# More tiles for rounded weight pieces, a product queue one shorter, and another order of first sums in an attention, expert and gated kernel

## The chip, the cores and the metric

The kernel runs on one core of one Trainium2 chip. The metric is the device time of one execution in microseconds (us); lower is better. Shown times are medians of several runs, and one further execution was recorded by the hardware profiler. Engines are written as the profile writes them: PE (TensorE matmuls), PEld (its weight loads), DVE (VectorE), ACT (ScalarE), POOL (GpSimd), SP (the queue that issues most DMAs).

## The reference

Three layers follow one another; float32 in and out (the weights come as float64, their bits are taken apart on the chip).

```python
# 1. attention with sigmoid weights: 4 batches, 12 heads, 448 tokens, 64 per head
scores = scale * np.matmul(q, k.transpose(0, 1, 3, 2)) - np.log(S)
x = np.matmul(1 / (1 + np.exp(-scores)), v)      # -> 1792 tokens x 768
# 2. top-1 mixture of 8 experts, 768 -> 1024 -> 768, routed by cosine similarity
out[mask] = gate_w[mask, None] * (np.maximum(x[mask] @ w1[e], 0) @ w2[e])
# 3. gated layer, 768 -> 1536 -> 768: the last part of the kernel
a = x @ w_a
b = x @ w_b
return (a * b @ w_out).astype(np.float32)
```

## The kernel before

The change lies in the last part, the function `glu`. The 1792 rows of x go through it in two groups of 896 rows (`G` = 2). For each group, first the two products x @ w_a and x @ w_b are made and multiplied for 12 slices of 128 hidden columns (`ab`, one call for each slice, `f`), and the result is sent to DRAM (`m_d`). Then `out_part` multiplies it with `w_out` in two passes of 12 steps each (`k` from 0 to 23): four blocks of 128 rows in the first pass, three in the second.

**Splitting.** A float32 product is made of three matmuls of rounded pieces. `split` does it: ACT casts the source to the high piece (L718), DVE subtracts it from the source to get the low piece (L719).

**Seven products.** The two products of one slice are done by a scheme with seven block products instead of eight (`NPROD` = 7). `combo(n)` prepares the weight operand of product n: for product 1 two sums in a row, for products 3 and 6 one sum each (`sum_`, L1020, on DVE), for products 0, 2, 4 and 5 none, and then a split. Product 6's combo also starts the load of a later weight slice (`w_load`, L1009, on SP). The operands lie in a pool of 10 `w` tiles; `ab` prepares each operand `AHEAD` = 8 products before it is used, at the head of the product's turn in the loop. Since the scheme has seven products, in product j of `ab` the combo of number (j + 1) mod 7 stands. After each product DVE takes sums out of PSUM: `u2` after product 1 (L1061), `u3` after product 3 (L1066, L1067), `c21` and half of `m` after product 5 (L1072, L1073), the rest after product 6 (L1079, L1080). Three PSUM banks serve seven products (`BANK`), so product 3 may begin only when `u2` has been read, and product 5 when `u3` has.

**The right-hand operand.** `y_combo(g, c)` makes one column block (of seven) of x's group g: six transposes on PE, one copy `k1` on ACT (L981), two casts on ACT (L987, L988), four first sums on DVE into `ts` (L989 to L992), a cast of these on ACT (L993), and three subtractions on DVE (L995 to L997). The seven columns of group 0 are made one after the other ahead of the first `ab`, a combo behind each. Those of group 1 are made inside `out_part(0)` at the steps k in `rows_at`, a row load (`y_next`) some steps ahead of each.

**Rounded pieces of w_out.** While `ab` runs for group 0, `prep_more` is called in product 2 and in product 5 of each slice. A call stores what an earlier call finished (`prep_store`, L218, on SP), finishes the unit of an earlier call on DVE (`prep_finish`, L211), starts a load, and begins a new unit (`prep_unit`): two steps on DVE (L195, L197), two on ACT (L199, and L201, an absolute value written into a tile `ab`), one addition on POOL (L202). A unit is finished two calls after it was begun and stored three calls after. There are three `ab` tiles, so the unit begun in that third later call writes the tile which the store issued in that same call is reading.

Each engine takes its instructions in the order in which the program issues them (a schedule by hand), and waits on semaphores.

Of the kernel before, what the change touches and what calls it, by code (L numbers as in the profile page):

```python
# [9 lines left out]
F32 = mybir.dt.float32  # L10
F32R = mybir.dt.float32r
# [13 lines left out]
def build(ctx: ExitStack, tc: tile.TileContext, q, k, v, emb, tau, w1, w2, wa, wb, wo, out, dbg=None, stop=None):  # L25
# [6 lines left out]
    nc = tc.nc  # L32
# [4 lines left out]
    P = 128  # L37
# [6 lines left out]
    HD = DM // 2  # L44
# [19 lines left out]
    prep_p = prep_s.enter_context(tc.tile_pool(name="prep", bufs=1))  # L64
# [8 lines left out]
    G = len(PHASES)  # L73
# [91 lines left out]
    HU = DM // 2  # L165
    units = [(f, part, hf) for parts in ((0, 1), (2,)) for f in range(NF) for part in parts for hf in range(2)]
    next_unit, unit_end = [0], [4 * NF]
    prep_raw = {}
    prep_sum, prep_out = [], []

    def prep_load(u, dma=nc.sync):
        if u >= unit_end[0]:
# [12 lines left out]
    def prep_unit():  # L185

        u = next_unit[0]
        if u not in prep_raw:
            return
        next_unit[0] += 1  # L190
        t = prep_raw.pop(u)
        top, low = t[:, :, 1], t[:, :, 0]
        t16 = t.rearrange("p n t -> p (n t)").bitcast(BF16).rearrange("p (n t) -> p n t", t=4)[:, :, 3]
        m = prep_p.tile([P, HU], I32, tag="m", name="m", bufs=2)
        nc.vector.tensor_scalar(out=m, in0=top, scalar1=3, scalar2=0x3FFFFFFF,  # L195
                                op0=ALU.logical_shift_left, op1=ALU.bitwise_and)
        nc.vector.scalar_tensor_tensor(out=m, in0=top, scalar=-0x40000000, in1=m,  # L197
                                       op0=ALU.bitwise_and, op1=ALU.bitwise_or)
        nc.scalar.activation(out=low, in_=low.bitcast(U32), func=AF.Copy, scale=2.0 ** -29)  # L199
        ab = prep_p.tile([P, HU], F32, tag="ab", name="ab", bufs=3)  # L200
        nc.scalar.activation(out=ab, in_=t16, func=AF.Abs)  # L201
        nc.gpsimd.tensor_tensor(out=m, in0=m, in1=low, op=ALU.add)  # L202
        prep_sum.append((u, m, ab))
# [479 lines left out]
    HP = P // 2  # L683
    yg = {}

    def y_load(g, c, tiles):

        w = DM // len(tiles)
        for h in range(2):
            r0 = Y0 * (1 - g) + (h * NC + c) * HP  # L690
            for hf, t in enumerate(tiles):
                nc.sync.dma_start(out=t[h * HP:(h + 1) * HP, :], in_=ys_d[r0:r0 + HP, hf * w:(hf + 1) * w])
        yg[g, c] = tiles if len(tiles) == 2 else [tiles[0][:, :HD], tiles[0][:, HD:]]
# [15 lines left out]
    def transpose_raw(px, t, k0, n):  # L709

        px = px.bitcast(F32R)
        t = t.bitcast(F32R)
        for kk in range(n):
            nc.tensor.transpose(out=px[:, kk * P:(kk + 1) * P], in_=t[:, (k0 + kk) * P:(k0 + kk + 1) * P],
                                identity=ident_r)
# [228 lines left out]
    def glu():  # L944
# [4 lines left out]
        def pool(name, bufs, **kw):  # L949
            return gs.enter_context(tc.tile_pool(name=name, bufs=bufs, reuse_waits="tile", **kw))  # L950

        g_p = pool("g", 1)
        ps_o = pool("ps_o", 1, space=PSUM)
        ps_y = pool("ps_y", 2, space=PSUM)
        KH = KD // 2
        HN = NC * HP
        B11, B21, B22, T1, T2, T3, T4 = range(7)
# [1 line left out]
        RHS = [B11, T2, T1, T3, B21, T4, B22]  # L959
        BANK = [0, 1, 2, 1, 0, 1, 2]  # L960
        NPROD = 7
        AHEAD = 8
        NS = G * NF
        bt = [g_p.tile([P, 7, KH, HN], F32R, name=f"bt{h}") for h in "hl"]

        def tmp(tag, n, bufs, nm, dt=F32):
            return g_p.tile([P, 512], F32, tag=tag, name=nm, bufs=bufs)[:, :n]

        def acc_ps(k):
            return [ps_o.tile([P, 512], F32, tag=f"o{3 * k + j}", name=f"o{3 * k + j}") for j in range(3)]  # L970


        def y_combo(g, c, px=None):

            px = [ps_y.tile([P, 512], F32, tag="py", name="py") for _ in range(2)] if px is None else px
            hv = yg.pop((g, c))
            k = [t[:, :HD] for t in px]
            for hf in range(2):
                transpose_raw(k[hf], hv[hf], 0, KH)
            k1 = tmp("c21", HD, 1, "k1")  # L980
            nc.scalar.copy(out=k1, in_=k[0])  # L981
            v = [a.rearrange("p (k h q) -> p h k q", k=KH, h=2) for a in (k1, k[1])]
            t = g_p.tile([P, 4, KH, HP], F32, tag="ts", name="ts", bufs=1)
            cs = slice(c * HP, (c + 1) * HP)
            sub = ALU.subtract
            bh, bl = (b[:, :, :, cs] for b in bt)
            nc.scalar.copy(out=bh[:, B11], in_=v[0][:, 0])  # L987
            nc.scalar.copy(out=bh[:, B21:B22 + 1], in_=v[1])  # L988
            nc.vector.tensor_tensor(out=t[:, 0], in0=v[0][:, 1], in1=v[0][:, 0], op=sub)  # L989
            nc.vector.tensor_tensor(out=t[:, 1], in0=v[1][:, 1], in1=t[:, 0], op=sub)  # L990
            nc.vector.tensor_tensor(out=t[:, 2], in0=v[1][:, 1], in1=v[0][:, 1], op=sub)
            nc.vector.tensor_tensor(out=t[:, 3], in0=v[1][:, 0], in1=t[:, 1], op=sub)  # L992
            nc.scalar.copy(out=bh[:, T1:], in_=t)  # L993
            bf = bh.bitcast(F32)
            nc.vector.tensor_tensor(out=bl[:, B11], in0=v[0][:, 0], in1=bf[:, B11], op=sub)  # L995
            nc.vector.tensor_tensor(out=bl[:, B21:B22 + 1], in0=v[1], in1=bf[:, B21:B22 + 1], op=sub)
            nc.vector.tensor_tensor(out=bl[:, T1:], in0=t, in1=bf[:, T1:], op=sub)  # L997

        def y_next(g, c):
            t = g_p.tile([P, DM], F32, tag="yr", name="yr", bufs=2)  # L1000
            y_load(g, c, [t])


        def w_raw(i):
            return r2[0][:, 2 * (i % 4):2 * (i % 4) + 2, :]
# [7 lines left out]
        def combo(n):  # L1013
            i, j = divmod(n, NPROD)
            r = w_raw(i)
            a1, a2, b1, b2 = (r[:, s, hf * HD:(hf + 1) * HD] for s in range(2) for hf in range(2))

            def sum_(k, x, y, op):
                t = g_p.tile([P, HD], F32, tag=f"s{min(k, 3)}", name=f"s{k}", bufs=1)
                nc.vector.tensor_tensor(out=t, in0=x, in1=y, op=op)  # L1020
                sums[k] = t

            if j == 1:
                sum_(1, b1, b2, ALU.add)
                sum_(2, sums[1], a1, ALU.subtract)
            elif j == 3:
                sum_(3, a1, b1, ALU.subtract)
            elif j == 6:
                sum_(4, a2, sums[2], ALU.subtract)
            src = sums[S_OF[j]] if S_OF[j] else {0: a1, 4: a2, 5: b2}[j]  # L1030
            w = g_p.tile([P, 2, HD], F32R, tag="w", name="w", bufs=10)
            split(w[:, 0], w[:, 1], src, w[:, 0].bitcast(F32))
            wq[n] = w
            if j == NPROD - 1:
                w_load(i + 4)


        def ab(i):
# [6 lines left out]
            for j in range(NPROD):  # L1045
                n = i * NPROD + j
                if n + AHEAD < (g + 1) * NF * NPROD:
                    combo(n + AHEAD)
                w = wq.pop(n)
# [42 lines left out]
        op, accs = {}, []  # L1092
# [11 lines left out]
        def out_split(g, k):  # L1104
            if k < 2 * NF:
                mr, wr = op[g, k]
                n = mr.shape[-1]
                gh, gl = (tmp(tg, n, 2, nm).bitcast(F32R) for tg, nm in (("p1", "gh"), ("u2", "gl")))
                wh, wl = (g_p.tile([P, 2, HD], F32R, tag="w", name="w", bufs=10).rearrange("p a b -> p (a b)")
                          for _ in range(2))  # L1110
                split(gh, gl, mr, gh.bitcast(F32))
                split(wh, wl, wr, wh.bitcast(F32))
                op[g, k] = (gh, gl, wh, wl)
# [38 lines left out]

        def out_part(g):

            rows_at = {3: 0, 5: 1, 7: 2, 9: 3, 12: 4, 15: 5, 18: 6} if g + 1 < G else {}
            for k in range(2 * NF):
                out_load(g, k + 2) if k + 2 < 2 * NF else None
                out_split(g, k + 1)
                if rows_at and k < 2 * NF:
                    c = next((c for kk, c in rows_at.items() if kk == k + 3), None)  # L1160
                    if c is not None:
                        y_next(g + 1, c)
                out_mm(g, k)
                store(g)
                if k in rows_at:
                    y_combo(g + 1, rows_at[k])
                elif k < 3:
                    prep_more(g)
                if g + 1 < G and 14 <= k < 14 + AHEAD:
                    combo((g + 1) * NF * NPROD + k - 14)  # L1170

        for i in range(4):
            w_load(i)
        y_next(0, NC - 1)
        for c in range(NC):
            y_combo(0, c, acc_ps(c % 3)[:2] if c % 3 < 2 else None)
            combo(c)
        unit_end[0] = len(units)
        for u in range(next_unit[0], next_unit[0] + 3):
            prep_load(u)  # L1180
        for n in range(NC, AHEAD):
            combo(n)
# [50 lines left out]
```

## Time and profile before

| | us |
|---|---|
| median of 3 runs | 1155.24 (1155.08 to 1155.33) |
| the profiled execution's own time | 1152.64 |
| its span in the profile | 1150.9 |
| PE busy | 1059.7 (92%) |
| DVE busy | 734.3 (64%) |
| ACT busy | 504.4 (44%) |
| mean granted TensorE clock | 0.962 of full speed |

Busy time of an engine is the share of the span in which it executes; instructions that only wait or issue a DMA are not counted. A row of a timeline gives start, duration, engine, line and operands, and in square brackets how long the engine sat idle just before and what released it. The granted clock is 1.00 at 2.4 GHz and 0.50 at 1.2 GHz. The part `glu` runs from about 553 us to the end.

### The profile page before, as it was taken

The page shows a single profiled execution, that of the slowest core. Times are in us where ns is not written, and L with a number is a line of the kernel's source. Part 1 is how long each engine was busy: PE and PEld are TensorE (multiplying, and loading weights), DVE is VectorE, ACT ScalarE, POOL GpSimd, SP SyncE. Part 2 cuts the span into 40 slices and gives each one's busy share as a digit, 9 for nine tenths or more (in the row PEclk, how much of TensorE's full clock was granted, in tenths as well). Part 3 has the DMA queues.
Part 4 walks back from the last instruction along what each step waited for, and adds up shares of the span by engine and source line. Part 5 has one row for each costly group of instructions (what it writes and reads, how often), then busy time and mean ns, then how long its engine had stood idle before and what let it go on. Part 6 is the DMA issues. An engine that isn't in the chain of part 4 may idle for free.

```text
span 1150.9 us, 17128 instructions
## 1 busy us (share of the span) xinstructions
PE 1059.7 (92%) x5780; PEld 876.2 (76%) x5780; DVE 734.3 (64%) x1399; ACT 504.4 (44%) x841; POOL 150.9 (13%) x218
## 2 busy tenths in 40 slices
PE   7999999999999999999468798889998999999998
PEld 4555555699888888898357687787886899998887
DVE  2465788756956695631586777775666677775444
ACT  5776677424845483512343323332544222232343
POOL 2121213132222222211001111110000000000000
PEclk9999999999999999999678988989998999999999
DMA  8577687546877687151433434436574222203564
GB/s 194 147 187 201 179 230 221 197 158 252 304 267 253 256 309 277 67 140 42 154 124 125 159 134 125 165 119 213 160 238 139 101 88 107 78 37 127 166 208 150
DMA packets 129468, 195.58 MB, mean 170 GB/s; under 512 B 52040, under 2 KB 92616, under 8 KB 129360
## 3 DMA queue, kind: packets, MB, share of 16 engines
q1 hardware_dynamic: 125392, 179.14, 48.8%
q0 software_dynamic: 3040, 14.94, 3.4%
q8 instruction: 47, 0.77, 0.3%
q14 instruction: 61, 0.50, 0.1%
q10 hardware_dynamic: 928, 0.23, 0.1%
HBM read 151.02 MB, written 43.25 MB: 169 GB/s over the span
## 4 chain that ended last, share of the span: by engine, by line
PE 33%; DVE 8%; ACT 4%; DMA 3%; issue 3%; SPq 0%; DVEq 0%; ACTq 0%
PE o L1053 22%; PE o L1134 11%; DVE w L719 2%; DMA wo<-ab 2%; ACT w L718 2%; DVE s L1020 1%; ACT bth L993 1%; DVE btl L997 1%; DMA wr<-wo 1%; DVE u L1061 1%; DVE ts L990 0%; ACT k L981 0%; ACT p L1058 0%; DMA raw<-in_moe_w_out_dram 0%; DVE gl L719 0%
## 5 line engine op out<-in xcount | busy, mean ns | idle before, releaser
L1053 PE MATMUL o<-bth,w 128*128 128x448 f32 x1008 | 302.6, 380 | 36.8 <-DVE u L1061 27.5
L1053 PEld LDWEIGHTS o<-bth,w 128*128 128x128 f32 x1008 | 198.5, 197 | 58.7 <-issue 30.7
L1053 PE MATMUL o<-btl,w 128*128 128x448 f32 x504 | 191.0, 379 | 1.1 <-DVE btl L995 1.1
L1134 PE MATMUL o<-w,gh 128*128 128x512 f32 (+1 forms) x672 | 174.8, 349 | 11.5 <-ACT w L718 6.5
L1134 PEld LDWEIGHTS o<-w,gh 128*128 128x128 f32 x672 | 118.2, 194 | 32.8 <-DVE w L719 10.5
L202 POOL TENSOR_TENSOR m<-m,raw 128x384 int32<-128x384 int32 x72 | 74.8, 1039 | 496.8 <-DVE m L197 233.7
L718 ACT CAST w<-s 128x384 fp32r<-128x384 f32 x96 | 49.2, 513 | 196.4 <-DVE s L1020 176.1
L1134 PE MATMUL o<-w,gl 128*128 128x512 f32 x336 | 116.9, 348 | 1.4 <-DVE gl L719 1.4
L1053 PEld LDWEIGHTS o<-btl,w 128*128 128x128 f32 x504 | 99.4, 197 | 9.9 <-DVE btl L995 1.5
L530 ACT ACTIVATE a<-ps,bias_s 112x896 f32<-112x896 f32 x96 | 91.6, 1005 | 30.8 <-PE ps L529 30.4
L719 DVE TENSOR_TENSOR w<-s,w 128x384 fp32r<-128x384 f32 x96 | 53.6, 558 | 54.4 <-ACT w L718 54.4
L780 PE MATMUL p<-w1h,xl 128*128 128x512 f32 x216 | 85.3, 395 | 2.6 <-DVE xl L719 2.6
L778 PE MATMUL p<-w1h,xh 128*128 128x512 f32 x216 | 86.6, 401 | 0.1
L779 PE MATMUL p<-w1l,xh 128*128 128x512 f32 x216 | 84.6, 392 | 0.0
L541 PE MATMUL av<-a,v 112*64 112x448 f32 x384 | 82.5, 552 | 0.0
L864 PE MATMUL p<-w2h,hTl 128*128 128x384 f32 x288 | 74.1, 338 | 8.3 <-DVE hTl L719 8.3
L201 ACT ACTIVATE ab<-raw 128x384 f32<-128x384 bf16 x72 | 39.8, 553 | 90.3 <-DMA wo<-ab 46.4
L864 PE MATMUL p<-w2h,hTh 128*128 128x384 f32 x288 | 76.2, 345 | 0.0
L719 DVE TENSOR_TENSOR hTl<-px,hTh 128x512 fp32r<-128x512 f32 x35 | 24.1, 688 | 81.4 <-ACTq L845 68.1
L864 PE MATMUL p<-w2l,hTh 128*128 128x384 f32 x288 | 73.6, 336 | 0.0
L1134 PEld LDWEIGHTS o<-w,gl 128*128 128x128 f32 x336 | 65.3, 194 | 10.3 <-DVE gl L719 2.6
L719 DVE TENSOR_TENSOR gl<-mr,gh 128x512 fp32r<-128x512 f32 (+1 forms) x48 | 29.9, 623 | 50.1 <-ACT gh L718 49.8
(246 smaller groups left out, 1771.9 us busy)
## 6 DMA issues: line engine op xcount, KB each, us to landing
r<-in_moe_w_dram SPq DMA_DIRECT2D x28, 768.0 KB, 7.8
r<-in_moe_w_dram SPq DMA_DIRECT2D x18, 1024.0 KB, 6.2
r<-wab SPq DMA_DIRECT2D x24, 768.0 KB, 4.4
wr<-wo SPq DMA_DIRECT2D x48, 384.0 KB, 3.6
m<-mm SPq DMA_DIRECT2D x24, 448.0 KB, 2.5
raw<-in_moe_w_a_dram SPq DMA_DIRECT2D x24, 384.0 KB, 3.5
raw<-in_moe_w_b_dram SPq DMA_DIRECT2D x24, 384.0 KB, 5.0
wab<-ab SPq DMA_DIRECT2D x48, 192.0 KB, 3.7
```

The lines of the kernel that those rows point to most:

```text
L201: nc.scalar.activation(out=ab, in_=t16, func=AF.Abs)
L202: nc.gpsimd.tensor_tensor(out=m, in0=m, in1=low, op=ALU.add)
L530: nc.scalar.activation(out=a[:, c2], in_=ps[:, :, :S], func=AF.Sigmoid, bias=bias_s[:CP], scale=qscale)
L541: nc.tensor.matmul(t[j * D:(j + 1) * D, :S], lhsT=raw[i, "v"][:, j, c, :], rhs=a[:, c2, j, :], start=c == 0, stop=c == NCH - 1)
L718: nc.scalar.copy(out=hi, in_=src)
L719: eng.tensor_tensor(out=lo, in0=src, in1=f32_hi, op=ALU.subtract)
L778: nc.tensor.matmul(ps, lhsT=xh[:, kk, :], rhs=w1h[kk][:, cs], start=kk == 0, stop=False)
L779: nc.tensor.matmul(ps, lhsT=xh[:, kk, :], rhs=w1l[kk][:, cs], start=False, stop=False)
L780: nc.tensor.matmul(ps, lhsT=xl[:, kk, :], rhs=w1h[kk][:, cs], start=False, stop=kk == KD - 1)
L864: nc.tensor.matmul(yp[hf][:, :HD], lhsT=l[:, kk, :], rhs=wv[kk][:, hf * HD:(hf + 1) * HD], start=kk == 0 and wv is w2h and l is hTh, stop= ...
L1053: nc.tensor.matmul(bank[BANK[j]], lhsT=w[:, l, ks], rhs=bt[r][:, RHS[j], kk, :], start=j < 3 and kk + l + r == 0, stop=kk == KH - 1 and l ...
L1134: nc.tensor.matmul(t[:, z0:z0 + d1 - d0], lhsT=l[:, cs], rhs=r[:, d0:d1], start=first and z == 0, stop=last and z == 2)
```

## The change

Five things are done together.

- Two more tiles for the absolute values (`ab2`, in another pool), used by two units of every five in the last part, so that a tile is used again after five units and not three.
- `AHEAD` is 7 and not 8, and there are 9 `w` tiles and not 10. In product j of `ab` now the combo of number j stands.
- `y_combo` is divided into `y_sums` (transposes, copy, casts, first sums) and a rest (cast of the sums, three subtractions). Ahead of group 0's products the rest of a column is issued behind the first sums of the next one; `k1` and the sums alternate between two tiles for that.
- Group 1's columns are made at steps 1, 3, 5, 7, 9 of the first pass and 12, 16 of the second, instead of 3, 5, 7, 9 and 12, 15, 18. The first row load is issued at the head of `out_part`.
- At step 1 a column stands where `prep_more` stood.

```diff
@@ prep_unit
-        ab = prep_p.tile([P, HU], F32, tag="ab", name="ab", bufs=3)
+        ab = (prep_p.tile([P, HU], F32, tag="ab", name="ab", bufs=3) if not more_ab or u % 5 < 3 else
+              more_ab[0].tile([P, HU], F32, tag="ab2", name="ab2", bufs=2))
@@ glu
-        AHEAD = 8
+        AHEAD = 7
@@ y_combo, now y_sums, which returns rest
-            k1 = tmp("c21", HD, 1, "k1")
+            k1 = tmp(*(("c21", HD, 1, "k1") if c % 2 else ("p1", HD, 2, "k1")))
-            t = g_p.tile([P, 4, KH, HP], F32, tag="ts", name="ts", bufs=1)
+            t = g_p.tile([P, 4 * KH * HP if ts == "ts" else 2 * HN], F32, tag=ts, name=ts, bufs=1)
+            t = t[:, :4 * KH * HP].rearrange("p (s k q) -> p s k q", s=4, k=KH)
-            nc.scalar.copy(out=bh[:, T1:], in_=t)
...
+            def rest():
+                nc.scalar.copy(out=bh[:, T1:], in_=t)
+                nc.vector.tensor_tensor(out=bl[:, B11], in0=v[0][:, 0], in1=bf[:, B11], op=sub)
+                nc.vector.tensor_tensor(out=bl[:, B21:B22 + 1], in0=v[1], in1=bf[:, B21:B22 + 1], op=sub)
+                nc.vector.tensor_tensor(out=bl[:, T1:], in0=t, in1=bf[:, T1:], op=sub)
@@ combo, and the same in out_split
-            w = g_p.tile([P, 2, HD], F32R, tag="w", name="w", bufs=10)
+            w = g_p.tile([P, 2, HD], F32R, tag="w", name="w", bufs=9)
@@ out_part
-            rows_at = {3: 0, 5: 1, 7: 2, 9: 3, 12: 4, 15: 5, 18: 6} if g + 1 < G else {}
+            rows_at = {1: 0, 3: 1, 5: 2, 7: 3, 9: 4, 12: 5, 16: 6} if g + 1 < G else {}
+            if rows_at:
+                y_next(g + 1, 0)
@@ ahead of group 0's products
+        rest = None
         for c in range(NC):
-            y_combo(0, c, acc_ps(c % 3)[:2] if c % 3 < 2 else None)
+            px = acc_ps(c % 3)[:2] if c % 3 < 2 else [ps_y.tile([P, 512], F32, tag="py", name="py") for _ in range(2)]
+            nxt = y_sums(0, c, px, "mm" if c % 2 else "ts")
+            if rest:
+                rest()
             combo(c)
+            rest = nxt
+        rest()
         unit_end[0] = len(units)
+        more_ab.append(g_p)
```

## Rows read from the trace of the kernel before

**Rows 1.** Busy times by stretch: PE, PEld, DVE, ACT, POOL, granted clock, DMA

```profile
586.00:787.00 201.00, 173.13 (x755) 154.27 (x756) 145.31 (x276) 65.64 (x141) 24.50 (x23) 0.91 0.43 144
902.00:1057.00 155.00, 154.64 (x763) 142.79 (x762) 114.06 (x207) 41.84 (x91) 0.00 (x0) 1.00 0.22 82
```

**Rows 2.** Waits of PE from 586 us on: total us, times, longest

```profile
PE o L1053 <- DVE u L1061: 27.5, 11, 3.8
```

**Rows 3.** Waits of ACT, 586 to 800 us

```profile
ACT ab L201 <- DMA wo<-ab: 46.4, 12, 4.2
```

**Rows 4.** Timelines of SP, ACT and DVE within one slice of group 0

```profile
665.67 0.43 SPq L218 DMA_DIRECT2D wo<-ab  x1
670.53 0.55 ACT L201 ACTIVATE ab<-raw 128x384 f32<-128x384 bf16 x1 [4.23 <-DMA wo<-ab]
667.00 0.62 DVE L1072 TENSOR_TENSOR c<-o,p 128x448 f32<-128x448 f32 x1 [0.57 <-PE o L1053]
671.52 0.56 DVE L719 TENSOR_TENSOR w<-r,w 128x384 fp32r<-128x384 f32 x1 [1.78 <-ACT w L718]
676.31 0.62 DVE L1061 TENSOR_TENSOR u<-o,p 128x448 f32<-128x448 f32 x1
```

**Rows 5.** Timeline of PE, first matmuls after idle time, group 0

```profile
593.39 0.47 PE L1053 MATMUL o<-bth,w 128*128 128x448 f32 x1 [0.24 <-DVE u L1061]
642.39 0.44 PE L1053 MATMUL o<-bth,w 128*128 128x448 f32 x1 [2.01 <-DVE u L1061]
646.43 0.47 PE L1053 MATMUL o<-bth,w 128*128 128x448 f32 x1 [0.16 <-DVE u L1066]
677.07 0.44 PE L1053 MATMUL o<-bth,w 128*128 128x448 f32 x1 [2.67 <-DVE u L1061]
764.28 0.71 PE L1053 MATMUL o<-bth,w 128*128 128x448 f32 x1 [3.18 <-DVE u L1061]
```

**Rows 6.** Busy times by stretch, as in the first group: three stretches behind idle time

```profile
678.10:681.60 3.50, 3.50 (x12) 3.07 (x11) 3.40 (x7) 1.64 (x4) 1.11 (x1) 0.51 0.00 0
764.30:770.30 6.00, 6.00 (x16) 5.35 (x17) 4.90 (x10) 2.24 (x5) 1.11 (x1) 0.50 0.04 15
870.10:876.40 6.30, 6.30 (x20) 5.08 (x21) 3.78 (x6) 2.03 (x5) 0.00 (x0) 0.52 0.59 187
```

**Rows 7.** Timeline of DVE within one slice of group 1

```profile
957.39 0.62 DVE L1061 TENSOR_TENSOR u<-o,p 128x448 f32<-128x448 f32 x1
...
962.02 0.55 DVE L1020 TENSOR_TENSOR s<-r,s 128x384 f32<-128x384 f32 x1
963.23 0.56 DVE L719 TENSOR_TENSOR w<-s,w 128x384 fp32r<-128x384 f32 x1 [0.66 <-ACT w L718]
964.01 0.62 DVE L1072 TENSOR_TENSOR c<-o,p 128x448 f32<-128x448 f32 x1 [0.22 <-PE o L1053]
...
968.84 0.56 DVE L719 TENSOR_TENSOR w<-s,w 128x384 fp32r<-128x384 f32 x1 [0.66 <-ACT w L718]
...
970.15 0.62 DVE L1061 TENSOR_TENSOR u<-o,p 128x448 f32<-128x448 f32 x1
```

**Rows 8.** Timelines of POOL and DVE, group 0

```profile
669.97 1.03 POOL L202 TENSOR_TENSOR m<-m,raw 128x384 int32<-128x384 int32 x1 [6.01 <-DMA wo<-ab]
775.75 1.03 POOL L202 TENSOR_TENSOR m<-m,raw 128x384 int32<-128x384 int32 x1 [7.17 <-DVE m L197]
776.09 1.17 DVE L1080 TENSOR_TENSOR mm<-u,u 128x448 f32<-128x448 f32 x1
```

**Rows 9.** Timeline of PE in the output part of group 0

```profile
814.58 0.62 PE L1134 MATMUL o<-w,gh 128*128 128x512 f32 x2 [0.37 <-DVE w L719]
870.10 0.80 PE L1134 MATMUL o<-w,gh 128*128 128x512 f32 x1 [3.39 <-ACT w L718]
884.36 0.49 PE L1134 MATMUL o<-w,gh 128*128 128x512 f32 x1 [1.22 <-ACT w L718]
```

**Rows 10.** Timeline of DVE ahead of group 0's products

```profile
571.04 0.96 DVE L997 TENSOR_TENSOR btl<-ts,bth 128x768 fp32r<-128x768 f32 x1 [0.16 <-ACT bth L993]
```

More of the change, by code (lines that the diff above doesn't have):

```diff
@@ L168, in build @@
     prep_raw = {}
-    prep_sum, prep_out = [], []
+    prep_sum, prep_out, more_ab = [], [], []
     def prep_load(u, dma=nc.sync):
@@ L970, in acc_ps, with y_combo, y_sums @@
             return [ps_o.tile([P, 512], F32, tag=f"o{3 * k + j}", name=f"o{3 * k + j}") for j in range(3)]
-        def y_combo(g, c, px=None):
+        def y_combo(g, c, px=None, ts="ts"):
+            y_sums(g, c, px, ts)()
+        def y_sums(g, c, px, ts):
             px = [ps_y.tile([P, 512], F32, tag="py", name="py") for _ in range(2)] if px is None else px
@@ L992, in y_combo @@
             nc.vector.tensor_tensor(out=t[:, 3], in0=v[1][:, 0], in1=t[:, 1], op=sub)
-            nc.scalar.copy(out=bh[:, T1:], in_=t)
             bf = bh.bitcast(F32)
-            nc.vector.tensor_tensor(out=bl[:, B11], in0=v[0][:, 0], in1=bf[:, B11], op=sub)
-            nc.vector.tensor_tensor(out=bl[:, B21:B22 + 1], in0=v[1], in1=bf[:, B21:B22 + 1], op=sub)
-            nc.vector.tensor_tensor(out=bl[:, T1:], in0=t, in1=bf[:, T1:], op=sub)
+            def rest():
[3 more added lines that the diff above has]
+                nc.vector.tensor_tensor(out=bl[:, T1:], in0=t, in1=bf[:, T1:], op=sub)
+            return rest
         def y_next(g, c):
@@ L1108, in out_split @@
                 gh, gl = (tmp(tg, n, 2, nm).bitcast(F32R) for tg, nm in (("p1", "gh"), ("u2", "gl")))
-                wh, wl = (g_p.tile([P, 2, HD], F32R, tag="w", name="w", bufs=10).rearrange("p a b -> p (a b)")
+                wh, wl = (g_p.tile([P, 2, HD], F32R, tag="w", name="w", bufs=9).rearrange("p a b -> p (a b)")
                           for _ in range(2))
```

## The prediction, made before the changed kernel ran

> **What bounds the kernel now.** I read the stretches first. In group 1's products PE is busy in 154.64 of 155 us at full clock; in group 0's products, the same matmuls, only in 173 of 201 us, at a clock of 0.91 [rows 1]. So group 0 is where time can be had. PE's waits name what it lacks there: `u2` (L1061), 27.5 us in 11 waits, always ahead of product 3 [rows 2]. `u2` is late because DVE is late, and DVE's timeline shows one long wait in a slice: 1.78 us for an ACT cast [rows 4]. ACT had stood for 4.23 us in front of its absolute value, until a store landed: the store left SP at 665.67 and ACT went on at 670.53 [rows 4]. There are 12 such waits, 46.4 us [rows 3]; most of one is covered, since DVE has other work, and what DVE feels is the 1.78.
>
> The slice has a cycle in group 0: `u2` on DVE, product 3 to 5 on PE, `c21` (L1072) on DVE, then DVE's work until the next `u2`. Its length sets the stage, not PE's work. From product 3 of slice 0 to that of slice 10 ten cycles take 764.28 - 593.39 = 170.9 us [rows 5], 17.1 each, where group 1 takes 970.15 - 957.39 = 12.76 [rows 7].
>
> **Part 1, five tiles.** A tile is now written two calls after its store was issued, most of a slice, against the 4.9 us from issue to release in rows 4: ACT's wait goes to nothing. What is late next is DVE itself. Without the 1.78 its way from `c21` to `u2` is 676.31 - 667.00 - 1.78 = 7.53 us [rows 4].
>
> **Part 2, `AHEAD` 7.** This moves each combo by one product against the PSUM work. Product 6's combo, with its sum, the wait for ACT and its subtraction, came ahead of `c21` and now comes behind it: 963.23 - 962.02 + 0.48 = 1.69 us more between `c21` and `u2`, where 0.48 is a 0.56 us subtraction less the overlap with its successor. Product 2's combo leaves: 970.15 - 968.84 - 0.48 = 0.83 less [rows 7]. So DVE's way from `c21` to `u2` grows by 0.86, and the way from `u2` to `c21` shrinks by as much, where it helps less, as PE is the slower there.
>
> On SP the weight load (L1009) moves from ahead of product 5's store to behind it; nothing queued waits for it, since it is three slices early. Nine `w` tiles for seven operands leave the same two to spare as ten for eight.
>
> *Group 1.* Behind the start of `u2` product 3 starts 0.76 later (676.31 to 677.07, [rows 4, 5]). PE then needs 27 matmuls of 12.76/63 = 0.2026 us and 0.2 for the last to drain, 5.68, to `c21`. DVE needs 970.15 - 964.01 = 6.14 from there to `u2` now [rows 7]; 6.14 + 0.86 - 0.16 (a small wait for PE that is absorbed) = 6.84 after. Cycle: now 0.76 + 5.68 + 6.14 = 12.58, less than PE's 12.76; after, 13.28. The stage turns from PE's to DVE's pace, and loses 0.52 in each of the ten slices behind the first that still prepare operands: **+5.2 us** (from 0, should the estimate of the slack be off by half a microsecond, to 6).
>
> *Group 0.* Product 3 to `c21`: 5.68, and product 5 waits for `u3` as now, 646.43 - 642.39 - 18 x 0.2026 = 0.39 [rows 5]. `c21` to `u2`: 7.53 + 0.86 = 8.39. Cycle 0.76 + 6.07 + 8.39 = 15.22. Two things stretch it.
>
> One is POOL's addition. Now it starts at 669.97, in the 1.78 us in which DVE stands [rows 4, 8]. That pause goes, and product 6's sum and subtraction move there. Where the addition did meet a DVE step with two operands in SBUF, the step took 1.17 instead of 0.62, until just behind the addition's end [rows 8]. I take 0.35 for the second call and 0.2 for the first, of bounds 0 and 0.55 each: cycle 15.77. (The Trainium skill, SBUF — State Buffer, Terms, says that DVE and GpSimd arbitrate for one port pair, exclusively for a whole instruction, so that the loser fully blocks. The rows bear it out. It speaks against the change: the removed wait hid the addition. By the rule without overlap elsewhere the cycle would be 15.77, by rows that show no such meeting at this place 15.22.)
>
> The other is the clock. Behind an idle stretch of 2.67 us ahead of product 3 the granted clock is 0.51 for 3.5 us, so 1.7 us of PE's time is lost [rows 5, 6]. Behind 2.01 us 18 matmuls took 4.04, so it stayed at 2.4 GHz [rows 5]. After, the idle is 15.77 - 12.76 - 0.4 = 2.6, or 2.1 at 15.22: between the two. And now a fall hurts more: DVE reaches `c21` earlier and waits for PE in full. With a fall the cycle is 0.76 + 7.38 + 8.39 + 0.35 = 16.88. I take a fall in one slice of three: **16.1**.
>
> Ten cycles: the first has no finishing steps, 1.1 shorter; 9 x 16.1 + 15.0 = 159.9, a gain of 11.0. The eleventh has no combos; it loses only 6 us at half clock, 3.0 us, now [rows 6], of which I take 2.5 as gained. Group 0: **-13.5 us** (bounds: 15.22 gives -22.3, 16.88 with no more than 2.5 gives -5.7).
>
> **Part 3, the first sums.** Ahead of group 0's products DVE waits 0.16 in each of seven columns for the cast of the sums [rows 10]; issuing the rest behind the next column's sums hides that, 1.1 us at most. But the last column's rest now stands behind product 6's combo (1.69 us of DVE), and PE's second matmul needs it. The two cancel: **0** (-1.1 to +0.6). `k1` in a tile of `p1` waits for nothing more: inside `out_part` the other user of that tag, the high piece, comes behind it in ACT's queue, and `k1`'s last reader is done by then. Were that wrong, each of four columns would cost a cast and a subtraction, some 1.2 us.
>
> **Part 4, the columns.** In the second pass a step has a quarter less PE work to hide a column. The one at step 15, beside product 1's two sums, costs a 3.39 us stall [rows 9], and then 6.3 us at a clock of 0.52 [rows 6], 3.0 lost: 6.4. The one at step 18, beside a combo without a sum, costs 1.22, one in the first pass 0.37 [rows 9]. The new step 16 falls beside product 2's combo, without a sum: I price it as step 18's. So 6.4 goes and 0.37 comes at step 1; the two sums alone at step 15 may cost 0.3, and nine `w` tiles hold two of the last steps back instead of one, 0.5. The first row load takes SP 1.1 us ahead of the third step's loads; PE's running step covers it. `prep_more` gone from step 1 costs nothing, step 2 stores the last units, and these are read only at the end of the pass. **-5.2 us** (-6.5 to 0).
>
> **Sum.** -13.5 + 5.2 + 0 - 5.2 = -13.5. The profiled execution took 1152.64 (span 1150.9), 2.6 below the median; differences are put to the median: 1155.24 - 13.5 = **1141.7**.
>
> **Rivals.**
> *A, free clock.* The addition meets nothing and the clock stays up: cycle 15.22, group 0 -22.3, total 1155.2 - 22.3 = 1133. For: 2.1 us idle is nearer to the 2.01 that left the clock alone. Against: the meeting in rows 8.
> *B, clock falls in each slice.* 16.88: -5.7 + 5.2 - 5.2, 1149.5. For: it falls behind 2.67 us [rows 5, 6].
> *C, slower.* At 764.28 PE idled 3.18 us and then ran 6 us at half clock [rows 5, 6]; now that costs little, as DVE is late too. After, with product 5's `c21` waiting for PE, 3.0 lost in each slice gives 0.76 + 8.68 + 8.39 + 0.35 = 18.2 a cycle: 9 x 18.2 + 17.1 = 180.9, +10; total 1165. It decides where the idle ahead of product 3 reaches 3.2 us; I expect 2.1 to 2.6.
> *D, group 1 keeps PE's pace.* Then 5.2 less: 1136.5. For: the slack is known to some tenths only.
> *E, the wait stays,* since something other than the tile holds ACT: group 0 gains nothing, about 1155. Against: in rows 4 the absolute value follows the store's landing.
>
> **How the numbers follow.** Forecast 0.38, A 0.22, D 0.12, B 0.18, C 0.06, E 0.04. The range leaves out C, E, and the ends of A and B: 1130 to 1151. About 0.2% (2.3 us) is what a measurement of this kernel can tell from no change. Faster by more than that: forecast, A, D and B, 0.90; same: E, 0.04; slower: C, 0.06.
>
> **What would show it.** ACT's wait for `wo<-ab` gone; `u2` to `u2` near 16 us in group 0, with DVE waiting for PE at `c21`; PE waiting about 0.5 us for `u2` in ten slices of group 1, where it never did, and a cycle of 13.3; the 3.39 us stall of the second pass gone, one near 1.2 left. If group 1 still runs at 12.76, part 2 is wrong; if L1080 or product 6's subtraction doesn't lengthen beside POOL, the collision is.

## The result, and the profile of the changed kernel

| | before | changed |
|---|---|---|
| median, us | 1155.28 (1155.08 to 1155.88) | 1142.16 (1138.21 to 1146.12) |
| profiled execution / its span | 1152.64 / 1150.9 | 1141.0 / 1139.3 |
| mean granted clock | 0.962 | 0.975 |

The ratio is 0.9886, with a 95% interval of 0.985 to 0.9921: faster by 13.1 us between the medians, where 13.5 was forecast, and by 11.6 between the two profiled executions. The lines have moved: `u2` is L1070, `u3` L1075 and L1076, `c21` L1081, the rest of the sums L1088 and L1089, a combo's sum L1029, the cast and the subtraction of a split L719 and L720, the products' matmuls L1062, those of the output part L1143. By stage, in the two profiled executions, from landmarks that both have:

| stage | before | changed | difference | forecast |
|---|---|---|---|---|
| last scaling of the expert part to product 0's second matmul | 33.42 | 35.42 | +2.0 | 0 |
| product 3 of slice 0 to that of slice 11 | 186.49 | 170.24 | -16.25 | -13.5 |
| from there to group 1's first `u2` | 125.75 | 121.25 | -4.5 | -5.2 |
| group 1, first `u2` to last `c21` | 147.75 | 153.81 | +6.1 | +5.2 |
| all else | | | +1.1 | 0 |

Busy times by stretch, the columns as in rows 1; the last two rows are the 3.5 us behind two starts of product 3:

```profile
588.00:774.00 186.00, 166.47 (x756) 147.89 (x756) 143.98 (x276) 63.68 (x140) 25.60 (x23) 0.95 0.46 155
884.00:1045.00 161.00, 157.93 (x763) 141.83 (x762) 112.47 (x208) 44.41 (x92) 0.00 (x0) 1.00 0.21 79
...
657.50:661.00 3.50, 3.50 (x12) 3.12 (x13) 2.78 (x7) 1.17 (x4) 1.11 (x1) 0.63 0.39 143
673.90:677.40 3.50, 3.48 (x17) 3.27 (x18) 2.77 (x7) 1.17 (x4) 1.13 (x1) 1.00 0.39 150
```

Against rows 1, group 0 has become shorter and still has PE idle for 19.5 us; group 1, where PE hardly stood (0.4), now has 3.1 us of idle time shown. Of "all else", 0.5 us is PE's half clock at the start, which lasts longer: from product 0's second matmul to product 3 of slice 0 it takes 7.74 instead of 7.24. The waits of PE and DVE (total us, times, longest), the last row for the kernel before:

```profile
PE o L1062 <- DVE u L1070: 20.3, 19, 1.9
...
DVE c L1081 <- PE o L1062: 14.0, 12, 2.4
...
DVE c L1072 <- PE o L1053: 7.8, 9, 2.4
```

ACT has no wait for `wo<-ab` left (rows 3: 46.4 us). PE's wait for `u2` has not gone: it is ten waits of 1.3 to 1.9 in group 0, where rows 2 have 11 of 2.5, and nine of 0.2 to 0.4 in group 1, which had none. DVE's wait for PE ahead of `c21` has grown. Ahead of the last slice of group 0 it was 0.2 to 1.3 in eight slices; now it is 0.6 behind a clock that stays up and 1.6 to 1.7 behind one that falls. In group 1 it was 0.2 and is 1.4 or 1.5. DVE's timeline shows both kinds in two slices of group 0, and then one slice of group 1:

```profile
656.74 0.62 DVE L1070 TENSOR_TENSOR u<-o,p 128x448 f32<-128x448 f32 x1
...
664.81 0.62 DVE L1081 TENSOR_TENSOR c<-o,p 128x448 f32<-128x448 f32 x1 [1.65 <-PE o L1062]
...
668.68 0.65 DVE L720 TENSOR_TENSOR w<-s,w 128x384 fp32r<-128x384 f32 x1 [0.66 <-ACT w L719]
...
673.16 0.62 DVE L1070 TENSOR_TENSOR u<-o,p 128x448 f32<-128x448 f32 x1
...
680.22 0.62 DVE L1081 TENSOR_TENSOR c<-o,p 128x448 f32<-128x448 f32 x1 [0.61 <-PE o L1062]
...
688.56 0.62 DVE L1070 TENSOR_TENSOR u<-o,p 128x448 f32<-128x448 f32 x1
...
915.46 0.62 DVE L1070 TENSOR_TENSOR u<-o,p 128x448 f32<-128x448 f32 x1
...
921.97 0.62 DVE L1081 TENSOR_TENSOR c<-o,p 128x448 f32<-128x448 f32 x1 [1.43 <-PE o L1062]
...
928.77 0.62 DVE L1070 TENSOR_TENSOR u<-o,p 128x448 f32<-128x448 f32 x1
```

From `u2` to `u2` the first slice takes 16.42 us and the second 15.40: one clock fall more. From `c21` to `u2` it is 8.35 and 8.34. Group 1's cycle is 13.31.

### The profile page after: what moved, and what is told of

Same layout as the page of the kernel before. It is cut to its first block, busy times and chain, and to the rows that moved or that the text cites. A ratio compares the mean times of both kernels' runs of the same rounds, so it can differ in the third digit from the quotient of the medians.

```text
span 1139.3 us, 17142 instructions
## 1 busy us (share of the span) xinstructions
PE 1051.3 (92%) x5780; PEld 864.9 (76%) x5780; DVE 730.9 (64%) x1399; ACT 505.3 (44%) x841; POOL 152.7 (13%) x218
## 4 chain that ended last, share of the span: by engine, by line
PE 26%; DVE 15%; ACT 4%; issue 3%; DMA 2%; SPq 0%; ACTq 0%; DVEq 0%
PE o L1062 15%; PE o L1143 11%; DVE w L720 5%; ACT w L719 3%; DVE s L1029 3%; DMA wr<-wo 1%; DVE u L1088 1%; DVE u L1070 1%; DVE m L197 1%; DVE ab L212 1%; DVE c L1081 1%; DVE m L195 1%; ACT bth L1001 1%; DVE btl L1004 1%; DMA r<-wab 0%
## 5 line engine op out<-in xcount | busy, mean ns | idle before, releaser
L1062 PE MATMUL o<-bth,w 128*128 128x448 f32 x1008 | 300.3, 375 | 23.9 <-DVE u L1070 20.3
L1062 PEld LDWEIGHTS o<-bth,w 128*128 128x128 f32 x1008 | 194.2, 193 | 49.7 <-ACT raw L199 21.1
L1062 PE MATMUL o<-btl,w 128*128 128x448 f32 x504 | 188.2, 373 | 5.9 <-DVE btl L1002 5.9
L1143 PE MATMUL o<-w,gh 128*128 128x512 f32 (+1 forms) x672 | 171.3, 344 | 10.9 <-DVE w L720 5.7
L719 ACT CAST w<-s 128x384 fp32r<-128x384 f32 x96 | 47.0, 512 | 218.5 <-DVE s L1029 163.7
L1143 PEld LDWEIGHTS o<-w,gh 128*128 128x128 f32 x672 | 115.5, 190 | 32.6 <-DVE w L720 12.2
L1143 PE MATMUL o<-w,gl 128*128 128x512 f32 x336 | 115.3, 343 | 1.4 <-DVE gl L720 1.4
L1062 PEld LDWEIGHTS o<-btl,w 128*128 128x128 f32 x504 | 97.1, 193 | 14.4 <-DVE btl L1002 6.3
L720 DVE TENSOR_TENSOR w<-s,w 128x384 fp32r<-128x384 f32 x96 | 55.4, 577 | 47.4 <-ACT w L719 47.4
L720 DVE TENSOR_TENSOR hTl<-px,hTh 128x512 fp32r<-128x512 f32 x35 | 24.1, 688 | 81.6 <-ACTq L846 67.7
L1143 PEld LDWEIGHTS o<-w,gl 128*128 128x128 f32 x336 | 63.9, 190 | 10.0 <-DVE gl L720 2.6
L719 ACT CAST gh<-mr 128x512 fp32r<-128x512 f32 (+1 forms) x48 | 27.2, 566 | 79.0 <-PE o L1143 44.2
L865 PEld LDWEIGHTS p<-w2h,hTl 128*128 128x128 f32 x288 | 51.8, 188 | 10.3 <-DVE hTl L720 10.3
```

What stands on the lines that cost most here:

```text
L719: nc.scalar.copy(out=hi, in_=src)
L720: eng.tensor_tensor(out=lo, in0=src, in1=f32_hi, op=ALU.subtract)
L865: nc.tensor.matmul(yp[hf][:, :HD], lhsT=l[:, kk, :], rhs=wv[kk][:, hf * HD:(hf + 1) * HD], start=kk == 0 and wv is w2h and l is hTh, stop= ...
L1062: nc.tensor.matmul(bank[BANK[j]], lhsT=w[:, l, ks], rhs=bt[r][:, RHS[j], kk, :], start=j < 3 and kk + l + r == 0, stop=kk == KH - 1 and l ...
L1143: nc.tensor.matmul(t[:, z0:z0 + d1 - d0], lhsT=l[:, cs], rhs=r[:, d0:d1], start=first and z == 0, stop=last and z == 2)
```

## The experiments

They ask four things: what ended ACT's wait, what the shorter queue costs, what the other parts bring, and what bounds group 0's cycle in the end. They ran on several chips, each beside the kernel before (medians 1152.65 to 1153.98 there). A ratio is to that one. The changed kernel itself ran only for the first section, so a difference to it is better taken from the ratios than from the medians.

### What ended ACT's wait: five tiles, or something else?

**Five tiles alone**, in the kernel before:

```diff
-        ab = prep_p.tile([P, HU], F32, tag="ab", name="ab", bufs=3)
+        ab = (prep_p.tile([P, HU], F32, tag="ab", name="ab", bufs=3) if not more_ab or u % 5 < 3 else
+              more_ab[0].tile([P, DM], F32, tag="ot", name="ot", bufs=3)[:, :HU])
...
+        more_ab.append(g_p)
```

The two further tiles are output tiles (`ot`), which stand idle meanwhile. In this run and the next, `k1` also alternates between its two tiles, as in the change.

> The kernel before with five tiles alone (the two more are borrowed from the output tiles, which stand idle during group 0's products): AHEAD 8, ten operand tiles, columns and first sums as before. Both theories: the ACT wait goes, DVE's way from u2 to c21 is 7.46 us and from c21 to u2 7.53, a cycle of 15.0 to 15.6; group 1 keeps 12.77. Gain 9 x 2.1 + 2 = 17 to 23 us: 1132 to 1138, below the changed kernel. If the time is above 1142, five tiles need the shorter queue too, and the price of group 1 is not what the order costs.

Measured: 1131.28 (1126.87 to 1132.98), ratio 0.9814 (0.9783 to 0.9846). One of five parts, alone, is better than all five, by 8 us if the ratios are compared and by 11 if the medians are. ACT doesn't wait for `wo<-ab`, and DVE's timeline has one cycle throughout:

```profile
667.28 0.62 DVE L1070 TENSOR_TENSOR u<-o,p 128x448 f32<-128x448 f32 x1
674.74 0.62 DVE L1081 TENSOR_TENSOR c<-o,p 128x448 f32<-128x448 f32 x1
682.35 0.62 DVE L1070 TENSOR_TENSOR u<-o,p 128x448 f32<-128x448 f32 x1
```

15.07 us, 7.46 to `c21` and 7.61 back, with no wait for PE on either: DVE's own chain, its waits for ACT's casts included, is the cycle. PE idles 1.64 to 1.66 ahead of product 3 in nine slices, and its clock stays at 1.00 from 600 to 745 us:

```profile
600.00:745.00 145.00, 127.82 (x609) 112.56 (x608) 120.76 (x232) 52.14 (x116) 21.21 (x19) 1.00 0.49 165
...
668.05 0.44 PE L1062 MATMUL o<-bth,w 128*128 128x448 f32 x1 [1.65 <-DVE u L1070]
```

**The queue of seven alone** (`AHEAD` 7, nine `w` tiles, three `ab` tiles, old first sums and columns):

```diff
-        AHEAD = 8
+        AHEAD = 7
...
-            w = g_p.tile([P, 2, HD], F32R, tag="w", name="w", bufs=10)
+            w = g_p.tile([P, 2, HD], F32R, tag="w", name="w", bufs=9)
```

> The kernel before with AHEAD 7 and nine operand tiles alone: three tiles, columns and first sums as before. Theory T: the ACT wait stays as it is, product 6's sum comes behind c21, and both groups get slower: group 1 by 6 us, group 0 by nothing to 8, total 1161 to 1169. Theory O: group 0's cycle falls from 17.4 to 15.4 to 16.4 us, 15 us gained; group 1 goes from 12.77 to 13.31, 6 us lost; total about 1146.

Measured: 1145.8 (1141.99 to 1147.15), ratio 0.9928 (0.9907 to 0.995). **The changed kernel with three tiles** (the first diff turned round):

> The changed kernel with three tiles for the absolute values again; all else as changed. Theory T (the tiles make group 0's gain): ACT stands some 4 us for the store in each slice again, DVE feels 1.8 us of it, group 0's cycle goes from 15.4 to 16.4 us up to 17.2 or more, the time from 1142 to 1155 or more. Theory O (the order makes it: with a queue of seven the store of product 5 leaves SP ahead of the weight load instead of behind it, and ACT's next cast is not due for some 5 us behind the absolute value): ACT waits 1.5 to 3 us for the store, but nothing behind it is late; the time stays within 2 us of 1142.

Measured: 1142.4 (1140.78 to 1144.45), ratio 0.9901 (0.9872 to 0.9931), as with five. ACT's waits in these two, in this order, then SP's timeline in the second:

```profile
ACT ab L201 <- DMA wo<-ab: 12.0, 11, 4.5
```

```profile
ACT ab L201 <- DMA wo<-ab: 12.2, 11, 4.7
...
659.50 0.32 SPq L218 DMA_DIRECT2D wo<-ab  x1
...
668.23 0.32 SPq L1017 DMA_DIRECT2D r<-wab  x1
```

So the queue of seven ends most of the wait with three tiles, and five add nothing to it. The store of the second call leaves at 659.50 and no longer stands behind the weight load, which leaves 8.7 us later. In the kernel before the load came first; its waits and its timeline on SP, and DVE's last step on the tile of the store behind it:

```profile
SPq L1009 <- DVE s L1020: 114.8, 12, 26.8
...
665.30 0.32 SPq L1009 DMA_DIRECT2D r<-wab  x1
...
661.07 0.55 DVE L211 SCALAR_TENSOR_TENSOR ab<-ab,m 128x384 f32<-128x384 f32 x1
```

The load waits for a sum on DVE, and the store of rows 4, at 665.67, was the next in the queue. Its tile had been finished at 661.62: it stood for 4 us behind the load, and had not been late by itself.

**One DMA moved**, in the kernel before: that load is issued behind the call of `prep_more`.

```diff
             if j == NPROD - 1:
-                w_load(i + 4)
+                late.append(i + 4)
...
                     prep_more(g)
+                    while late:
+                        w_load(late.pop(0))
```

> The kernel before, with one DMA in another place: the load of a later weight slice, which product 6's combo issues on SP, is issued behind the second call of prep_more in the same slice, and so behind its store. Three tiles, AHEAD 8, the old first sums and the old column steps stay. Theory Q, SP's order: in the kernel before the load waits on SP for DVE's sum (114.8 us in 12 waits of SP from 586 to 787 us) and holds the store of an absolute value that was ready long before; a fifth of this is enough to make ACT late. Then the store leaves some 6 us earlier, ACT's wait for it falls from 46.4 to under 13 us, the cycle of group 0 is 15.1 us as with five tiles at AHEAD 8, and the time is 1131 (1127 to 1135). Theory T, too few tiles: a store issued in the same call as the tile's next use costs its landing, 4 us of ACT in a slice, wherever it stands: time 1153, cycle 17.1.

Measured: 1130.52 (1127.42 to 1135.87), ratio 0.9819 (0.9775 to 0.9862). ACT's wait and SP's timeline:

```profile
ACT ab L201 <- DMA wo<-ab: 5.6, 2, 3.8
...
656.88 0.32 SPq L218 DMA_DIRECT2D wo<-ab  x1
659.21 0.33 SPq L182 DMA_DIRECT2D raw<-in_moe_w_out_dram  x1
660.53 0.32 SPq L1009 DMA_DIRECT2D r<-wab  x1
```

That is the time of five tiles, with three. The cause of ACT's wait was SP's order, with a tile used again after three units; more tiles end the wait, and of its 46.4 us the moved load leaves 5.6 and the shorter queue 12.

### What the queue of seven costs

**The changed kernel with `AHEAD` 8** and ten `w` tiles (the two further `ab` tiles from the tag `ot`):

```diff
-        AHEAD = 7
+        AHEAD = 8
```

> The changed kernel with AHEAD 8 and ten operand tiles again (the two further tiles are borrowed from the output tiles); columns and first sums as changed. Theory (the shorter queue costs 6 us in group 1 and gives group 0 nothing that five tiles alone don't give): group 1's cycle 12.77, group 0's 15.06, total 1131 (five tiles alone) - 4.5 (columns) + 2 (first sums) = 1128.5. Rival (the parts don't add, for instance because columns and a longer queue collide in the second pass): above 1132.

Measured: 1125.78 (1123.4 to 1127.8), ratio 0.9756 (0.9718 to 0.9795): the shorter queue costs the change some 15 us, by the ratios. Group 1's timeline on DVE:

```profile
895.77 0.62 DVE L1081 TENSOR_TENSOR c<-o,p 128x448 f32<-128x448 f32 x1 [0.22 <-PE o L1062]
901.91 0.62 DVE L1070 TENSOR_TENSOR u<-o,p 128x448 f32<-128x448 f32 x1
...
908.53 0.62 DVE L1081 TENSOR_TENSOR c<-o,p 128x448 f32<-128x448 f32 x1 [0.22 <-PE o L1062]
```

6.14 us from `c21` to `u2` against 6.80 at seven, and a cycle of 12.76, PE's own, as in rows 7. Group 0's cycle is 15.06, against 15.85 on average in the change.

### First sums and columns

**Old first sums** in the changed kernel:

```diff
...
-            nxt = y_sums(0, c, px, "mm" if c % 2 else "ts")
-            if rest:
-                rest()
+            y_combo(0, c, acc_ps(c % 3)[:2] if c % 3 < 2 else None)
             combo(c)
...
```

> The changed kernel with the first sums of group 0's columns not pipelined (each column's rest before its combo, as before). In the changed kernel's trace product 0's second matmul starts 2.2 us later than before: 1.46 of it is DVE standing behind combo 0's cast, which waits for its weight load to land and now stands ahead of the first column's rest. Theory: undoing it gives 1.5 to 2.5 us back, about 1140. Rival (the late start is hidden by later waits, or is the landing of that load in this one run): within 0.5 us of 1142. Runs of the changed kernel spread over 8 us, so the trace decides: the start of product 0.

Measured: 1140.2 (1137.62 to 1142.59), ratio 0.9879 (0.9845 to 0.9914). The medians can't tell 2 us, the trace can: from the last expert scaling to product 0's second matmul it takes 33.39, against 35.42 in the change and 33.42 before. In the change, timelines of ACT, DVE and PE:

```profile
562.27 0.51 ACT L719 CAST w<-r 128x384 fp32r<-128x384 f32 x1 [3.38 <-DMA r<-wab]
...
562.82 0.56 DVE L720 TENSOR_TENSOR w<-r,w 128x384 fp32r<-128x384 f32 x1 [1.46 <-ACT w L719]
...
588.38 0.74 PE L1062 MATMUL o<-btl,w 128*128 128x448 f32 x1 [5.88 <-DVE btl L1002]
```

ACT's first combo waits for its weights; the first column's cast, which ran in that gap, now stands behind it, and DVE, which made the first column's subtractions meanwhile, stands for 1.46. And at the end the last column's rest stands behind product 6's combo: counted from the last scaling, PE's first matmul starts 2.8 us earlier than before, and then PE is idle for 5.88 (1.07 before).

**Old columns** in the changed kernel:

```diff
-            rows_at = {1: 0, 3: 1, 5: 2, 7: 3, 9: 4, 12: 5, 16: 6} if g + 1 < G else {}
-            if rows_at:
-                y_next(g + 1, 0)
+            rows_at = {3: 0, 5: 1, 7: 2, 9: 3, 12: 4, 15: 5, 18: 6} if g + 1 < G else {}
```

> The changed kernel with group 1's columns at the old steps (3, 5, 7, 9; 12, 15, 18) and the first row load where it was. Theory (a column beside product 1's two sums in the second pass costs a 3.4 us stall and a stretch at half clock): both come back, from product 3 of the last slice of group 0 to u2 of group 1's first slice 125.5 us instead of 121.3, total 1142 + 4 to 5 = 1146 to 1147. Rival (nine operand tiles already hold the second pass back, so that the step of the column no longer matters): within 1 us.

Measured: 1146.46 (1143.74 to 1149.64), ratio 0.9936 (0.9914 to 0.9959): 4.3 us slower than the change by the medians, 5.8 by the ratios; in the traces the way from group 0's last `u2` to group 1's first takes 128.71 against 122.71. PE's timeline, here and then in the change:

```profile
860.02 0.50 PE L1143 MATMUL o<-w,gh 128*128 128x512 f32 x1 [3.40 <-ACT w L719]
```

```profile
859.85 0.50 PE L1143 MATMUL o<-w,gh 128*128 128x512 f32 x1 [1.26 <-ACT w L719]
861.09 0.62 PE L1143 MATMUL o<-w,gh 128*128 128x512 f32 x2 [0.37 <-DVE w L720]
```

### What bounds the cycle: sums ahead of `c21`

**Early sums** in the changed kernel. A sum is followed by a cast on ACT and a subtraction on DVE, which waits 0.63 to 0.66 for the cast. Here the sums of products 3, 6 and the next slice's 1 are issued earlier, the latter two ahead of `c21`, the casts where they were (`combo(..., True)` issues the sum only):

```diff
+                soon = n + AHEAD + {4: 2, 5: 3}.get(j, 0)
+                if j in (4, 5) and soon < (g + 1) * NF * NPROD:
+                    combo(soon, True)
...
                     ve.tensor_tensor(out=u2, in0=Y, in1=p1, op=ALU.add)
+                    if n + AHEAD + 2 < (g + 1) * NF * NPROD:
+                        combo(n + AHEAD + 2, True)
```

> The changed kernel with the sums of products 3, 6 and 1 issued on DVE earlier: product 3's behind u2, product 6's behind product 4's combo and the next slice's two behind product 5's, all ahead of c21, where DVE stood waiting for PE; the casts and subtractions stay where they are. Theory (what sets the cycle is DVE's chain from c21 to u2, 8.35 us, of which 1.7 us are sums and 1.3 us their wait for ACT): the chain falls to about 5.4 us, the cycle 0.76 + 5.7 to 6.1 + 5.4 is below PE's 12.76 in both groups, PE sets the pace: group 0 gains 28 us, group 1 six, total 1106 to 1112. Rival (DVE's sum of work sets group 0's cycle, not the chain): DVE's busy 12.6 us a slice plus small waits, cycle 13.5 to 14.5, total 1112 to 1124; group 1 at 12.77 in either case.

Measured: 1109.07 (1105.84 to 1111.65), ratio 0.9613 (0.9576 to 0.9651). Busy times by stretch in both groups, and DVE's timeline in group 0:

```profile
590.00:745.00 155.00, 153.63 (x754) 141.89 (x753) 141.21 (x275) 66.13 (x138) 26.23 (x24) 0.99 0.55 182
890.00:1040.00 150.00, 149.25 (x757) 135.55 (x756) 98.13 (x174) 44.31 (x84) 0.00 (x0) 1.00 0.30 101
...
664.88 0.62 DVE L1093 TENSOR_TENSOR c<-o,p 128x448 f32<-128x448 f32 x1
...
670.33 0.62 DVE L1080 TENSOR_TENSOR u<-o,p 128x448 f32<-128x448 f32 x1
```

From `c21` to `u2` it is 5.45 instead of 8.35, and both groups run at 12.77 a slice. The 2.9 that went are three sums, 1.6, and two waits for their casts, 1.29. That pace is PE's own, as in rows 7, so the falls of the clock went too.

**The same with the old first sums**:

> The kernel of the early sums with the first sums of group 0's columns not pipelined. By the trace of the same edit on the changed kernel (33.4 instead of 35.4 us from the last expert block's scaling to product 0's second matmul): 2 us below the early sums.

Measured: 1110.56 (1104.15 to 1112.9), ratio 0.9603 (0.9554 to 0.9652). Not told from the run before it; in its profile the head is 33.3 us against 34.7, but the expert part had ended 5.6 us later, and group 0's 63 matmuls take 13.02 a slice instead of 12.77, with PE busy throughout and a granted clock of 1.00 in both. What made them slower is open.

**Early sums at `AHEAD` 8.** A first form issued each sum behind the last step of the product before:

```diff
+                soon = n + AHEAD + 1
+                if soon % NPROD in (1, 3, 6) and soon < (g + 1) * NF * NPROD:
+                    combo(soon, True)
```

> The changed kernel with AHEAD 8, ten w tiles and the two further tiles taken from another tag, and with the sums of products 1, 3 and 6 issued one combo early, behind the PSUM steps of the product before, so that ACT's cast of a sum has ended when its subtraction comes. If the waits of DVE for that cast on its way from c21 to u2 are what sets the cycle of group 0, both groups run at 12.8 us a slice and the time is that of the early sums at AHEAD 7, 1109 (1105 to 1112): the length of the queue is then worth nothing. If the queue of seven was needed for that pace, the cycle stays near 15.06 and the time at 1126. If AHEAD 8 still gains its 16 us on top, 1095 or less, which PE's busy time leaves no room for in the products (166 of 174 us).

Measured: 1126.94 (1122.18 to 1129.35), ratio 0.9767 (0.9731 to 0.9804). It says nothing on the question: the end of one product is directly ahead of the next one's head, so the order didn't change, and the run is a second one of `AHEAD` 8. Then the sums were moved, to a product's head, behind its combo:

```diff
+                soon = n + AHEAD + {0: 2, 4: 1, 5: 2}.get(j, 0)
+                if j in (0, 4, 5) and soon < (g + 1) * NF * NPROD:
+                    combo(soon, True)
```

> As the run before it (the changed kernel at AHEAD 8, ten w tiles, two tiles from another tag), whose edit put each sum only behind the last step of the product before, which in the program's order is directly ahead of its cast and subtraction, so that it moved nothing. Here the sums are really moved: product 6's to the head of product 4, product 1's two to the head of product 5, ahead of c21, product 3's to the head of product 0. From c21 to u2 DVE then has 5.45 us as in the early sums at AHEAD 7, and 0.55 more for product 3's sum, so 6.0; the cycle by the prediction's sum is 0.76 + 6.07 + 6.0 = 12.8, PE's own 12.77. If the waits for the cast of a sum set the cycle, both groups run at 12.8 and the time is 1109 (1105 to 1112). If the queue of seven was needed for it, 1126 as at AHEAD 8 without it.

Measured: 1107.83 (1106.98 to 1111.25), ratio 0.9614 (0.9578 to 0.965). So the length of the queue is worth nothing that the medians can tell once the sums are out of the way. Group 0's cycle is 13.23, all DVE's, as product 3's sum here stands between `c21` and `u2` (5.91 against 5.45 with the early sums at seven); group 1's is 12.77, and the way from group 0's last `u2` to group 1's first is 3.5 us shorter in this profile than in that one.

**No part of the change**, but the moved load and these sums in the kernel before:

> The kernel before with two edits of order alone: the weight load behind prep_more's store on SP, and the same early sums as in the run before this. Three tiles, AHEAD 8, old first sums, old column steps: no part of the change is in it. If order on SP and DVE holds all of the gain in the products, group 0 and group 1 run at 12.8 a slice; the columns cost their 4.3 us more and the first sums 1 to 2 less than in the early sums at AHEAD 7 (1109): 1112 (1108 to 1116). If the change's five tiles are needed once the cycle is 12.8, because a tile is then reused sooner than its store lands, ACT waits again for wo<-ab and the time is 1120 or more.

Measured: 1121.87 (1120.9 to 1124.26), ratio 0.9725 (0.9693 to 0.9758). Here the five tiles are missed. Waits and timeline of ACT, then DVE and POOL:

```profile
ACT ab L201 <- DMA wo<-ab: 17.5, 11, 3.8
...
668.16 0.56 ACT L201 ACTIVATE ab<-raw 128x384 f32<-128x384 bf16 x1 [1.34 <-DMA wo<-ab]
...
669.15 1.23 DVE L719 TENSOR_TENSOR w<-r,w 128x384 fp32r<-128x384 f32 x1 [0.46 <-ACT w L718]
...
668.93 1.03 POOL L202 TENSOR_TENSOR m<-m,raw 128x384 int32<-128x384 int32 x1 [4.57 <-ACT ab L201]
```

Group 0's cycle is 14.43 against 13.23 with five tiles, and nearly all of the difference is in these rows: 0.46 of waiting and a subtraction that takes 1.23 instead of 0.56, as ACT's wait has put POOL's addition beside it.

## Why the prediction was right, and where not

The time came out 0.5 us from the forecast. That closeness is luck: the changed kernel's own runs spread over 8 us, and the steps erred on both sides. What bounds the kernel was named rightly; the gain was put down to the wrong part.

- **What bounds the kernel.** Right in its views: group 0, `u2`, DVE, ACT, a store. It stopped one step short. The prediction took the store's start at 665.67 [rows 4] as the time at which it was ready; SP's waits would have shown that it stood behind the load, ready since 661.62. Rival E asked whether something other than the tile holds ACT, and was given 0.04 by the same reading.
- **Part 1.** ACT's wait went, as predicted, and the way from `c21` to `u2` without it is 7.61 with the tiles alone (7.53 forecast). But the credit was wrong: five tiles beside the shorter queue are worth nothing that the runs can tell. The prediction did move the load behind the store in part 2, and did not ask what that alone would do.
- **Part 2, the way from `c21` to `u2`.** 8.35 against 8.39 in group 0, 6.80 against 6.84 in group 1, and group 1's cycle 13.31 against 13.28: the step that was worked out most closely is the one that held best. (In group 0 the 8.39 is without POOL's addition and the 8.35 holds 0.09 of it: like for like it is 8.26.) The stage's sum was +6.1 and not +5.2, as the first two of its ten cycles paid 0.7 and 0.9 instead of 0.52, and the others 0.54 to 0.64.
- **Part 2, group 0's cycle.** Forecast 16.1, of 15.77 and 16.88 with a fall in one of three; measured 15.85, of 15.39 and 16.42 with a fall in four of nine. The way from `u2` to `c21` is as forecast (7.04 against 7.03 with the 0.2 for the first call); the 0.38 by which a cycle without a fall is shorter lies between `c21` and `u2`. POOL's addition was the mis-sized term: 0.35 was taken for the second call, 0.09 came (0.65 for 0.56 at 668.68). The prediction said that the pause in which the addition ran goes; product 6's combo brought another along, the 0.66 in which DVE waits for its cast, and the addition ran mostly there. Nine times 0.25 is 2.2 of the 2.7 us by which the stage beat its forecast; most of the rest is the first cycle, 14.2 on PE instead of 15.0. The clock's chance erred the other way, and by less. The idle ahead of product 3 was 1.85, under the 2.1 to 2.6 that were expected, and the clock fell behind it in four slices though it had stayed up behind 2.01 [rows 5]: the step that looked for the fall between 2.01 and 2.67 doesn't hold.
- **Rivals.** B, a fall in each slice, and A, none, were each true of some slices; D fell with group 1's cycle, C with idle times of 1.85 and a `c21` that waits at most 1.70 for PE in these slices; E fell with ACT's wait.
- **Part 3.** Forecast 0 (to +0.6), measured +2.0. The term that failed is what the first combo waits for: ACT stands 3.38 us for the weights of product 0, and the rest of the first column, which used that time, was put behind it, so that DVE stood for 1.46. The other 0.5 is in the prediction's own numbers, 1.69 less 1.1, which it called even. The waits of rows 10 are gone. The run with the old first sums undoes the whole part, so this division is read from the trace and not shown by a run.
- **Part 4.** -4.5 in the trace against -5.2; the 3.39 stall is gone, and 1.26 and 0.37 stand where 1.22 was priced.
- **What the prediction didn't see.** It priced `AHEAD` 7 against the kernel before. Priced against five tiles at `AHEAD` 8 it is the loss: some 8 us in group 0 (15.85 against 15.06 a slice) and 6 in group 1. A sum of parts gives the total; it doesn't show that one part undoes another. The same is true of the tiles, which are worth 22 us alone, none beside the shorter queue, and again 1.2 us a slice once the sums are early and the cycle is short.

## What to carry to other kernels

Where a transfer holds a buffer, follow it back one step further than its start: ask what stood ahead of it in its queue and what that waited for, before paying for more buffers. In a cycle of PSUM reads on one engine, list what stands between two reads and move out the pieces that wait for another engine's answer; here that took the changed kernel from 1142 to 1109 us. And price a part of a change against the other parts as well as against the kernel before.

## What the hardware showed

- **DVE beside POOL.** From 575 to 800 us in the traces of all 14 kernels, 211 DVE steps of 384 or 448 columns with both operands in SBUF began inside POOL's addition, and each ended 0.40 to 0.49 us behind that addition's end, whenever it began; 14 steps of 768 columns ended 0.81 to 0.82 behind it. A step that reads one operand from PSUM kept its 0.61 to 0.63 in 245 cases. The first two rows are of the change, the others of the kernel before:

```profile
667.78 1.13 POOL L203 TENSOR_TENSOR m<-m,raw 128x384 int32<-128x384 int32 x1 [7.17 <-DVE m L197]
668.68 0.65 DVE L720 TENSOR_TENSOR w<-s,w 128x384 fp32r<-128x384 f32 x1 [0.66 <-ACT w L719]
...
645.60 1.11 POOL L202 TENSOR_TENSOR m<-m,raw 128x384 int32<-128x384 int32 x1 [8.62 <-DVE m L197]
645.75 0.62 DVE L1066 TENSOR_TENSOR u<-o,p 128x448 f32<-128x448 f32 x1
```

So the price is what is left of the addition, less some 0.14: 0.09 with 0.23 left (668.68), 0.67 with 0.81 left in the last run (669.15 + 1.23 against 668.93 + 1.03), 0.55 with 0.69 left in rows 8 (776.09 + 1.17 against 775.75 + 1.03). That agrees with the Trainium skill (SBUF — State Buffer, Terms): the loser is blocked in full.

- **The clock's fall is not decided by the idle time in front alone.** In the change PE stood 1.85 ahead of product 3 both at 657.50 and at 673.92, and the granted clock behind it was 0.63 once and 1.00 the other time, the rows of the first section. With five tiles alone it stood 1.65 in nine slices and the clock stayed at 1.00. What tells the two slices at 1.85 apart is open.
